# Walking the columns of every split product backwards in an attention and mixture-of-experts kernel

## The chip, the cores and the metric

The kernel runs on one core of a Trainium2 chip. The metric is the device time of one execution in microseconds (us); the median of several executions counts.

## The reference

Three stages follow each other in float32: a block-causal attention (4 batches, 8 heads, 576 positions, head size 64), a gated product chain, and a layer with eight experts of which each token uses its best two.

```python
scores = scale * np.matmul(q, k.transpose(0, 1, 3, 2))      # scale = 1/8
scores = np.where(block_i >= block_j, scores, -1e9)         # blocks of 64 positions
attn = softmax(scores);  x = np.matmul(attn, v)             # -> x: 2304 tokens x 512
h = ((x @ w1) * (x @ w2)) @ w3                              # 512 -> 1024 -> 1024
y = h @ w_out                                               # 1024 -> 512
noisy = y @ w_gate + log1p(exp(y @ w_noise)) * noise        # 8 experts, top 2 per token
out[token] += weight * (relu(y @ w1[e]) @ w2[e])            # 512 -> 1024 -> 512, per expert
```

## The kernel before

Float32 accuracy comes from splitting. `split` writes a number as a high part (rounded by ScalarE into a tile of type float32r) and a low part (what is left, by VectorE or GpSimd). `mm3` then multiplies two split operands with three matmuls that add into one accumulator tile: high by high, high by low, low by high. In every `nc.tensor.matmul(out, a, c)` the second argument is the stationary operand, 128 columns that are loaded into TensorE ahead of time (PEld in the profile), and the third is the moving operand, whose columns stream past it; each moving column makes one output column in PSUM. In `mm3` the moving operand is `c` or `d` and the output is `out`, all three with columns that lie next to each other in memory.

All calls of `mm3`, by tile name in the profile:

- `w_unit`: the product of w3 and w_out, made once, tile `m` from `pc` and `pc`, 512 columns;
- `ab`: x by w1 and by w2, tile `m` from `xh` and `pc`, 256 columns, each of the two halves of one PSUM tile in turn;
- `yout`: the gated product by the combined matrix, tile `m` from `pc` and `gt`, 512 columns;
- `ffn1`: the first layer of an expert, tile `ph` from `xt` and `pc`, 384 columns for the first three slots of 128 tokens of an expert and 256 for the other two;
- `ffn2` and `last`: the second layer, tile `ph` from `pc` and `ht`, 512 columns, and 256 in the last call.

Matmuls that don't go through `mm3` are the attention's scores (`sb`), its transposes (`tp`), its products with v (`av`), the transposes of tokens (`m` from `ident`) and the router's small products.

The work of attention, of the product chain and of the experts is interleaved by hand-written strings of steps (`FIRST`, `LATER`) and by a scheduler that orders each engine's instructions when the program is built. PSUM accumulators come from pools of two to four buffers; ScalarE and VectorE read a finished accumulator and free it. In the last 420 us or so only the experts are left: `ffn1`, `ffn2`, transposes of gathered tokens, and scattered additions to the output by GpSimd's DMA queue.

Of the kernel before, what the change touches and what calls it, by code (L numbers as in the profile page):

```python
# [464 lines left out]
class Kernel:  # L465
# [17 lines left out]
    def mm3(self, out, lh, rh, first, last):  # L483
        nc = self.nc
        (a, b), (c, d) = lh, rh
        nc.tensor.matmul(out, a, c, start=first, stop=False)  # L486
        nc.tensor.matmul(out, a, d, start=False, stop=False)  # L487
        nc.tensor.matmul(out, b, c, start=False, stop=last)  # L488
# [661 lines left out]
```

## Time and profile before

| what | value |
|---|---|
| median of 3 runs | 1082.81 us (1082.0 to 1083.41) |
| profiled execution, its own time | 1085.02 us |
| its span, first to last instruction | 1083.2 us |
| granted TensorE clock, mean | 0.986 of full speed |
| PE busy (matmuls) | 1041.1 us, 96% of the span |
| PEld busy (loads of stationary operands) | 941.3 us, 87% |
| DVE, ACT, POOL busy | 555.8, 495.6, 299.7 us |

PE is TensorE, DVE is VectorE, ACT is ScalarE and POOL is GpSimd. A matmul's duration in the trace runs from its start to the modelled end of its last column, and matmuls overlap, so that the time between the starts of two neighbours is what a matmul costs the engine; that is read from the timeline.

### The profile page before, as it was taken

The numbers are of one execution on the slowest core, as the hardware profiler recorded it, in microseconds if no ns is written. First come the engines' busy times: TensorE is split into PE (matmuls) and PEld (weight loads), VectorE is DVE, ScalarE is ACT, GpSimd is POOL, SyncE is SP. The second block draws the span as 40 slices with busy tenths as digits, with TensorE's granted clock in tenths as the row PEclk, the third lists the DMA queues.
The fourth block names the chain that finished last, engine by engine and source line by source line (L and its number), as shares of the span: only waits on it lengthen the run. The fifth ranks groups of instructions, "written<-read, shape, count | busy, mean of one in ns | idle before, by whom it ended". The sixth has DMA issues, their size and how long they took to land.

```text
span 1083.2 us, 17428 instructions
## 1 busy us (share of the span) xinstructions
PE 1041.1 (96%) x6612; PEld 941.3 (87%) x6612; DVE 555.8 (51%) x1211; ACT 495.6 (46%) x1163; POOL 299.7 (28%) x307
## 2 busy tenths in 40 slices
PE   6999898999999999999999999999999999999994
PEld 4687687898899989899999889989898989898984
DVE  7898899585755656443345443533333433334110
ACT  5775566675666656522223433543333333333110
POOL 2000123135352426231444224330404131221111
PEclk9999998999999999999999999999999999999998
DMA  8664888237542563222323455663636354442221
GB/s 278 219 209 173 232 229 156 86 112 150 169 119 72 155 178 97 77 82 59 79 51 106 101 117 168 189 187 74 157 97 157 98 147 108 118 107 36 34 30 23
DMA packets 79250, 136.34 MB, mean 126 GB/s; under 512 B 21197, under 2 KB 46773, under 8 KB 78005
## 3 DMA queue, kind: packets, MB, share of 16 engines
q1 hardware_dynamic: 68901, 113.98, 36.6%
q0 software_dynamic: 10256, 21.16, 10.9%
q8 instruction: 54, 0.88, 0.3%
q14 instruction: 39, 0.32, 0.1%
HBM read 103.92 MB, written 31.19 MB: 125 GB/s over the span
## 4 chain that ended last, share of the span: by engine, by line
PE 86%; DMA 6%; DVE 3%; ACT 1%; issue 1%; POOL 1%; SPq 0%; POOLq 0%; ACTq 0%; DVEq 0%
PE ph L486 13%; PE ph L488 13%; PE ph L487 13%; PE m L486 10%; PE m L487 10%; PE m L488 10%; PE av L702 4%; PE tp L677 4%; PE sb L647 2%; PE sb L644 2%; DMA v<-in_v_dram 2%; PE m L959 2%; DMA stg<-in_w_dram 1%; DMA qk<-in_qk_dram 1%; PE m L244 1%
## 5 line engine op out<-in xcount | busy, mean ns | idle before, releaser
L486 PE MATMUL m<-xh,pc 128*128 128x256 f32 x576 | 165.0, 289 | 1.3 <-ACT pc L477 1.0
L487 PE MATMUL m<-xh,pc 128*128 128x256 f32 x576 | 163.0, 287 | 0.0
L488 PE MATMUL m<-xh,pc 128*128 128x256 f32 x576 | 162.0, 286 | 0.6 <-DVE nm L661 0.6
L487 PE MATMUL ph<-xt,pc 128*128 128x384 f32 (+1 forms) x512 | 157.0, 307 | 0.0
L488 PE MATMUL ph<-xt,pc 128*128 128x384 f32 (+1 forms) x512 | 157.0, 307 | 0.0
L486 PE MATMUL ph<-xt,pc 128*128 128x384 f32 (+1 forms) x512 | 156.5, 307 | 0.0
L976 DVE SCALAR_TENSOR_TENSOR ht<-ph,ht 128x384 fp32r<-128x384 f32 (+1 forms) x128 | 62.1, 490 | 154.6 <-ACT ht L975 150.5
L481 DVE TENSOR_TENSOR pc<-stf,pc 128x1024 fp32r<-128x1024 f32 (+1 forms) x75 | 88.1, 1190 | 91.3 <-ACT pc L477 85.0
L486 PE MATMUL ph<-pc,ht 128*128 128x512 f32 (+1 forms) x328 | 127.9, 390 | 0.0
L487 PE MATMUL ph<-pc,ht 128*128 128x512 f32 (+1 forms) x328 | 125.9, 384 | 0.0
L488 PE MATMUL ph<-pc,ht 128*128 128x512 f32 (+1 forms) x328 | 125.9, 385 | 0.0
L1022 POOL DMA_INDIRECT out_dram<-yo,ids x39 | 63.6, 1632 | 213.4 <-ACT yo L1018 110.0
L975 ACT ACTIVATE ht<-ph 128x384 fp32r<-128x384 f32 (+1 forms) x128 | 55.5, 438 | 133.3 <-PE ph L488 131.5
L486 PEld LDWEIGHTS m<-xh,pc 128*128 128x128 f32 x576 | 110.6, 193 | 2.8 <-ACT pc L477 1.2
L663 ACT ACTIVATE pb<-sb,nm 128x288 f32<-128x288 f32 (+3 forms) x192 | 94.1, 499 | 41.0 <-DVE nm L658 13.9
L487 PEld LDWEIGHTS m<-xh,pc 128*128 128x128 f32 x576 | 110.0, 192 | 0.6
L488 PEld LDWEIGHTS m<-xh,pc 128*128 128x128 f32 x576 | 109.4, 192 | 1.0 <-DVE pc L481 0.8
L481 POOL TENSOR_TENSOR gt<-at,gt 128x256 fp32r<-128x256 f32 x72 | 58.3, 815 | 149.6 <-ACT gt L477 149.2
L487 PEld LDWEIGHTS ph<-xt,pc 128*128 128x128 f32 x512 | 96.2, 188 | 0.5 <-DVE xt L481 0.2
L486 PEld LDWEIGHTS ph<-xt,pc 128*128 128x128 f32 x512 | 96.0, 188 | 0.5
L488 PEld LDWEIGHTS ph<-xt,pc 128*128 128x128 f32 x512 | 96.2, 188 | 0.0
L658 DVE TENSOR_REDUCE nm<-sb 128x1 f32<-128x128 f32 (+2 forms) x192 | 79.2, 439 | 28.5 <-PE sb L647 27.6
(160 smaller groups left out, 2163.5 us busy)
## 6 DMA issues: line engine op xcount, KB each, us to landing
stf<-in_m_dram SPq DMA_DIRECT2D x52, 512.0 KB
qk<-in_qk_dram SPq DMA_DIRECT2D x31, 576.0 KB
stg<-in_w_dram SPq DMA_DIRECT2D x14, 1024.0 KB
x<-ev SPq DMA_DIRECT2D x32, 288.0 KB
xab<-x SPq DMA_DIRECT2D x20, 256.0 KB
yt<-y SPq DMA_DIRECT2D x18, 260.0 KB
v<-in_v_dram SPq DMA_DIRECT2D x24, 160.0 KB
out_dram<-cst SPq DMA_DIRECT2D x3, 1280.0 KB
```

The costliest lines, as they stand in the source:

```text
L481: return d, eng.tensor_tensor(l, src, r32(h), op=OP.subtract)
L486: nc.tensor.matmul(out, a, c, start=first, stop=False)
L487: nc.tensor.matmul(out, a, d, start=False, stop=False)
L488: nc.tensor.matmul(out, b, c, start=False, stop=last)
L644: nc.tensor.matmul(o, lh, c.hi[:, 1, k0:k0 + w], start=True, stop=False)
L658: nc.vector.tensor_reduce(nm[:, n:n + 1], o[:, 0:w], axis=AX, op=OP.max, negate=True)
L663: nc.scalar.activation(pb[t][:, k0:k0 + src.free_size()], src, AF.Exp, bias=nm, scale=1.0, accum_out=sums[:, h // H, t + n, h % H:h % H + 1])
L677: nc.tensor.transpose(bank[:, n * P:(n + 1) * P], pb[t][:, kt * P:(kt + 1) * P], self.ident)
L702: nc.tensor.matmul(c.av[:, o0:o0 + w], c.vv[:, kt, :], c.pt[:, i, s0:s0 + w], start=(kt == 0 and i == 0), stop=(kt == 4 and i == m - 1))
L975: a = nc.scalar.activation(hh[:, 0, f, :], ph, AF.Relu)
L976: v = nc.vector.scalar_tensor_tensor(hh[:, 1, f, :], ph, 0.0, r32(hh[:, 0, f, :]), op0=OP.max, op1=OP.subtract)
L1022: nc.gpsimd.indirect_dma_start(out=self.a["out"], out_offset=self.idx(e, i), in_=yo, in_offset=None, compute_op=OP.add)
```

## The change

One line in `mm3` turns the views of the output and of the two moving operands round, so that each of its matmuls takes its moving columns from the last to the first and writes the output columns from the last to the first too. Column j of the moving operand still makes column j of the output. The stationary operands `a` and `b` are as before. The line sits ahead of the three matmuls, so that these are L487 to L489 in the changed kernel and L486 to L488 in the kernel before; later lines shift by one too.

```diff
     def mm3(self, out, lh, rh, first, last):
         nc = self.nc
         (a, b), (c, d) = lh, rh
+        out, c, d = out[:, ::-1], c[:, ::-1], d[:, ::-1]
         nc.tensor.matmul(out, a, c, start=first, stop=False)
         nc.tensor.matmul(out, a, d, start=False, stop=False)
         nc.tensor.matmul(out, b, c, start=False, stop=last)
```

In the built program the patterns of these matmuls begin at the last column and have a step of minus one where they had a step of one. Every engine has the same instructions in the same order as before. What differs beside the patterns is which of them wait for TensorE's own semaphore (`PE_49` in the rows). On TensorE, at the start of one chunk of `ab` (`y` holds the tokens that are transposed, `pc` the weights, `gt` the gated product), the kernel before has

```order
L487 MATMUL m<-pc_77,gt 128x512
L488 MATMUL m<-pc_77,gt 128x512
L235 MATMUL m<-ident,y 128x128 [waits Activation_49]
L235 MATMUL m<-ident,y 128x128 x3
L486 MATMUL m<-xh,pc_72 128x256
L487 MATMUL m<-xh,pc_72 128x256 [waits DVE_49]
L488 MATMUL m<-xh,pc_72 128x256
```

and the changed kernel has

```order
L488 MATMUL m<-pc_77,gt 128x512
L489 MATMUL m<-pc_77,gt 128x512
L235 MATMUL m<-ident,y 128x128 [waits Activation_49]
L235 MATMUL m<-ident,y 128x128 x3
L487 MATMUL m<-xh,pc_72 128x256 [waits PE_49]
L488 MATMUL m<-xh,pc_72 128x256 [waits DVE_49]
L489 MATMUL m<-xh,pc_72 128x256
```

The first matmul into a reused accumulator has gained a wait for an earlier matmul of TensorE itself, one that stands 19 instructions ahead of it; nothing has moved. There are 25 such added waits on TensorE, and the awaited matmul stands 6 to 75 instructions ahead of the waiting one. The other way round, 28 waits of this kind are gone, as at this place among the attention's scores, where the kernel before has

```order
L486 MATMUL m<-xh,pc_67 128x256
L487 MATMUL m<-xh,pc_67 128x256
L702 MATMUL av<-pt,vv 128x320 [waits Activation_49]
L488 MATMUL m<-xh,pc_67 128x256
L644 MATMUL sb<-hi 128x288 [waits PE_49,Activation_49]
L646 LDWEIGHTS mkl
```

and the changed kernel has

```order
L487 MATMUL m<-xh,pc_67 128x256
L488 MATMUL m<-xh,pc_67 128x256
L703 MATMUL av<-pt,vv 128x320 [waits Activation_49]
L489 MATMUL m<-xh,pc_67 128x256
L645 MATMUL sb<-hi 128x288 [waits Activation_49]
L647 LDWEIGHTS mkl
```

Here the matmul of the scores has lost its wait for TensorE and keeps the one for ScalarE.

## Rows read from the trace of the kernel before

**Rows 1.** The page: busy time by engine, and 40 slices of PE and clock.

```profile
PE 1041.1 (96%) x6612; PEld 941.3 (87%) x6612; DVE 555.8 (51%) x1211; ACT 495.6 (46%) x1163; POOL 299.7 (28%) x307
...
PE   6999898999999999999999999999999999999994
...
PEclk9999998999999999999999999999999999999998
```

**Rows 2.** The page: the chain that ended last, by engine, share of the span.

```profile
PE 86%; DMA 6%; DVE 3%; ACT 1%; issue 1%; POOL 1%; SPq 0%; POOLq 0%; ACTq 0%; DVEq 0%
```

**Rows 3.** Waits, longest in total: us, times, longest; first PE's, then ACT's.

```profile
PE tp L677 <- ACT pb L663: 6.3, 7, 1.7
PE sb L644 <- ACT hi L615: 5.5, 1, 5.5
...
ACT ht L975 <- PE ph L488: 131.5, 106, 3.8
```

**Rows 4.** PE by form, the first matmul of each triple; count, busy us, mean ns.

```profile
L486 PE MATMUL m<-xh,pc 128*128 128x256 f32 x576 | 165.0, 289 | 1.3 <-ACT pc L477 1.0 <-DVE at L212 0.2
...
L486 PE MATMUL ph<-pc,ht 128*128 128x512 f32 x312 | 123.3, 396 | 0.0
...
L486 PE MATMUL ph<-xt,pc 128*128 128x384 f32 x256 | 85.5, 337 | 0.0
...
L486 PE MATMUL ph<-xt,pc 128*128 128x256 f32 x256 | 70.9, 278 | 0.0
L486 PE MATMUL m<-pc,gt 128*128 128x512 f32 x144 | 56.4, 395 | 0.0
...
L486 PE MATMUL m<-pc,pc 128*128 128x512 f32 x64 | 25.5, 412 | 0.0
...
L486 PE MATMUL ph<-pc,ht 128*128 128x256 f32 x16 | 4.5, 283 | 0.0
```

**Rows 5.** Timeline of PE, first and last of unbroken runs: start us, modelled us, form.

```profile
576.97 0.28 PE L486 MATMUL m<-xh,pc 128*128 128x256 f32 x1
...
579.72 0.28 PE L486 MATMUL m<-xh,pc 128*128 128x256 f32 x1
...
899.92 0.34 PE L486 MATMUL ph<-xt,pc 128*128 128x384 f32 x1
...
916.39 0.34 PE L488 MATMUL ph<-xt,pc 128*128 128x384 f32 x1
...
973.61 0.28 PE L486 MATMUL ph<-xt,pc 128*128 128x256 f32 x1
...
984.38 0.28 PE L488 MATMUL ph<-xt,pc 128*128 128x256 f32 x1
...
1030.62 0.39 PE L486 MATMUL ph<-pc,ht 128*128 128x512 f32 x1
...
1046.71 0.39 PE L488 MATMUL ph<-pc,ht 128*128 128x512 f32 x1
1046.94 0.28 PE L486 MATMUL ph<-xt,pc 128*128 128x256 f32 x1
...
1058.13 0.28 PE L488 MATMUL ph<-xt,pc 128*128 128x256 f32 x1
```

**Rows 6.** Windows: stretch, length, busy us by engine, granted clock, DMA share, GB/s.

```profile
460.00:462.80 2.80, 2.80 (x15) 2.80 (x14) 0.00 (x0) 0.36 (x1) 0.00 (x0) 0.50 0.12 27
577.00:579.70 2.70, 2.70 (x25) 2.70 (x24) 0.11 (x1) 0.67 (x2) 1.60 (x2) 1.00 0.04 9
```

**Rows 7.** Timeline of PE in the first of these windows, first and last row.

```profile
460.04 0.41 PE L486 MATMUL m<-xh,pc 128*128 128x256 f32 x1
...
462.81 0.41 PE L487 MATMUL m<-xh,pc 128*128 128x256 f32 x1
```

**Rows 8.** The chain at the end of the program: start us, us, what.

```profile
1065.15 4.76 DMA out_dram<-yo,ids
...
1070.66 4.44 DMA out_dram<-ye,ids
```

## The prediction

> **What bounds the kernel now.** I read the page first. PE is busy for 96% of the span, and in the 40 slices it falls under eight tenths only in the first and the last one, while the granted clock stands near full nearly everywhere [rows 1]. The chain that ended last lies on PE for 86% of its length [rows 2]. The list of waits says the same from the other side: the longest wait of PE for anybody adds up to 6.3 us, whereas ScalarE waits 131.5 us for the matmuls of `ffn1` alone [rows 3]. So TensorE is the bound, and what a matmul costs it goes straight into the time. Only from 1065 us to the end at 1083 does the chain leave it, for two scattered additions to the output of 4.8 and 4.4 us one after the other [rows 8], which the change doesn't touch.
>
> The change alters no matmul but those of `mm3`, so I need their number and what one of them costs. The listing by form gives the first matmul of each triple [rows 4]; the other two have the same counts. With three per triple:
>
> - 256 columns, from `xh` in `ab` and the few of the last call: 3 x (576 + 16) = 1776;
> - 256 columns, from `xt`: 3 x 256 = 768;
> - 384 columns, from `xt`: 3 x 256 = 768;
> - 512 columns, in `ffn2`, `yout` and `w_unit`: 3 x (312 + 144 + 64) = 1560.
>
> That is 4872 of PE's 6612 matmuls. The mean duration in that listing is no price, because matmuls overlap. The price is the distance between starts in an unbroken run, from the timeline [rows 5]. From `xh`: 576.97 to 579.72 us holds 24 matmuls, so 2.75 us over 23 steps, 119.6 ns. 384 columns: 899.92 to 916.39, 96 matmuls, 16.47 over 95, 173.4 ns. 256 columns from `xt`: 973.61 to 984.38, 96 matmuls, 10.77 over 95, 113.4 ns. 512 columns: 1030.62 to 1046.71, 72 matmuls, 16.09 over 71, 226.6 ns. Together 1776 x 119.6 + 768 x 113.4 + 768 x 173.4 + 1560 x 226.6 ns = 212 + 87 + 133 + 354 = 786 us. Nearly three quarters of the span hang on the one property that the change touches: how fast TensorE takes and writes a run of columns.
>
> **The change part by part.** It removes no instruction and adds none, and no engine's order moves. It has two effects. First, 4872 matmuls read and write with a step of minus one. Second, a few waits differ.
>
> *The waits.* 25 matmuls now also wait for an earlier matmul of TensorE itself. What is queued behind such a matmul is all of PE's program, so a wait that holds would count in full. The awaited one stands at least 6 instructions ahead. At worst a waiting matmul would have to let its direct neighbour run out: the neighbour's modelled 0.39 us less the 0.227 us after which the next one starts anyway [rows 5], 0.16 us, which 25 times is 4 us. Since TensorE works in order and the awaited matmul lies several steps back, it has normally ended by then, so I take 0 and keep 4 us as the far end. The 28 waits that are gone were of the same already answered sort: the list of waits has none of PE for PE, and the largest entry of the matmul that loses most of them, `sb` at L644, is for ScalarE [rows 3]. They give back 0.
>
> *The walk.* No matmul of the kernel before has a step other than one in a moving operand or in an output, so the trace doesn't show the price, and I bound it.
>
> From above, by the nearest row in which a column takes longer. [...] In that stretch the same matmul from `xh` starts every 213.1 ns: 460.04 to 462.81 us, 14 matmuls, 13 steps [rows 7]. That is what 256 columns cost when each takes two ticks of the full clock. Scaled by columns it makes 319.7 ns for 384 and 426.2 ns for 512. If every backward column took two ticks, the change would add 1776 x 93.5 + 768 x 99.7 + 768 x 146.3 + 1560 x 199.6 ns = 166 + 77 + 112 + 311 = 666 us.
>
> From below: half of 213.1 is 106.6 ns, what 256 columns need at full clock and nothing more; for 384 and 512 it is 159.9 and 213.1. The prices above lie 13.0, 6.8, 13.5 and 13.5 ns over that. Were walking backwards to remove all of this, it would save 1776 x 13.0 + 768 x 6.8 + 768 x 13.5 + 1560 x 13.5 ns = 23 + 5 + 10 + 21 = 60 us. I see no reason why it should: the 13 ns are there whatever the length, so they belong to the change from one matmul to the next and not to the direction within one.
>
> Between these ends I take 0. What the rows show of a matmul's price is a number of columns at the clock plus a small constant: 384 columns cost 53 to 60 ns more than 256, and 512 cost 53 ns more than 384, against 53.3 ns for 128 columns by the half-clock row. A backward walk has the same columns, the same bytes and the same neighbours in memory: two columns that follow each other still lie next to each other, and the stream reaches each stretch of memory once. Only the order within it is turned, for reads and writes alike. [...]
>
> [...]
>
> The sum is then 0 for the walk, 0 for the added waits, 0 for the lost ones. Against the profiled execution that is 1085.0 us again; its own time lies 2.2 us over the median of the runs, 1082.8 us, so I forecast 1082.8 us.
>
> **The rivals.** *Two ticks per backward column.* [...] Then PE's share grows by 666 us, no other engine can hide any of it, since all wait for PE [rows 3], and the time is 1083 + 666 = 1749 us. It is the case that ends on the slower side, and it decides as soon as a backward column costs visibly more than a tick: each tenth of a tick more would be some 67 us. For it speaks that the operands are 4 bytes wide at a column per tick of the full clock, the heaviest stream that TensorE has in this kernel; against it, that the step changes no address but the order.
>
> *A few ns per matmul more.* The trace shows that a matmul's price isn't fixed to the ns. The same 96 matmuls of `ffn1` with 256 columns cost 113.4 ns each at 973.61 us and, with 1046.94 to 1058.13 us over 95 steps, 117.8 ns in the last expert [rows 5]. If a start at the far end of a row costs such a step of 4.4 ns, all 4872 pay 21 us, and the time is 1104 us.
>
> *A few ns less.* The same step in the other direction, where the turned order meets the loads of the stationary operand more favourably, gives 1083 - 21 = 1061 us. Against both small cases: the two blocks walk in the same direction and still differ, so that the direction is not what sets this step.
>
> That the change doesn't do what it says can be left out: the built program holds the step of minus one in all these matmuls.
>
> **How the numbers follow.** No effect: 0.60. Two ticks: 0.19. A few ns more: 0.11. A few ns less: 0.10. The predicted time is that of the first, 1082.8 us. The first, third and fourth hold 0.81 together, so the range goes from 1060 to 1106 us and leaves out the rival at 1749 us; the 4 us of waits lie within it. About 0.2% (2.2 us) is what a measurement of this kernel can tell from no change. Of the first case I give 0.02 to either side for a shift of a little over that. Faster: 0.10 + 0.02 = 0.12. Same: 0.56. Slower: 0.19 + 0.11 + 0.02 = 0.32.
>
> **What would show it.** In the changed kernel the steps between starts should again be 119 to 120, 173.4, 113 to 118 and 227 ns in unbroken runs of 256 (`xh`), 384, 256 (`xt`) and 512 columns, with PE's busy time near 1041 us and no PE wait above 7 us. Steps of about 213, 320 and 426 ns at full granted clock would prove the first rival, and then PE near 100% busy. Steps that all moved by the same few ns would prove one of the small ones, and a list with PE waiting at the first matmul of an accumulator would mean the waits weren't free. The prediction is wrong if columns written or read backwards are slower at all.

## The result, and the profile after

The changed kernel takes 1094.11 us (median of 4 runs, 1093.92 to 1096.24), the kernel before beside it 1082.4 us (1081.76 to 1083.41): a ratio of 1.0105 with a 95% interval from 1.0089 to 1.0121. It is 1% slower, and the forecast of no change was wrong, though the time lies within the range. Its profiled execution has a span of 1094.4 us, 11.2 us over that of before, at a mean granted clock of 0.984 against 0.986.

The page of the changed kernel shows the same picture as [rows 1, 2], with more busy time on the engine that bounds it:

```profile
PE 1053.9 (96%) x6612; PEld 947.1 (87%) x6612; DVE 556.4 (51%) x1211; ACT 494.8 (45%) x1163; POOL 301.3 (28%) x307
...
PEclk9999898999999999999999999999999999999998
...
PE 87%; DMA 4%; DVE 3%; issue 2%; ACT 2%; SPq 1%; POOL 1%; POOLq 0%; ACTq 0%; DVEq 0%
```

PE is busy for 12.8 us more, with the same 6612 matmuls, at a clock that fell under nine tenths of full in one slice more than before. The section on the change says that every engine has the same instructions as before; that isn't quite so. The page counts 17411 instructions where that of before counts 17428: sixteen of TensorE's semaphore instructions and one of VectorE's are gone, and all others stand in the same order. The list of PE's waits (us in total, times, longest) answers to [rows 3]:

```profile
PE sb L645 <- DVE hi L615: 7.7, 3, 5.5
PE sb L645 <- ACT pb L664: 4.6, 3, 3.3
PE tp L678 <- ACT pb L664: 4.5, 5, 1.6
```

In the same list of before, `hi` stands under two engines, ACT with 5.5 us [rows 3] and DVE with

```profile
PE sb L644 <- DVE hi L614: 2.1, 2, 1.1
```

together 7.6 us, so that the 7.7 us, which pass the prediction's mark of 7 us, are the same wait and not a new one. No wait of PE for PE is in the list, and all these are waits of the attention for its own operands, of about the size they had. So the 25 added waits don't show. The listing by form answers to [rows 4], for the first matmul of each triple:

```profile
L487 PE MATMUL m<-xh,pc 128*128 128x256 f32 x576 | 165.3, 290 | 1.1 <-ACT pc L477 1.0
...
L487 PE MATMUL ph<-pc,ht 128*128 128x512 f32 x312 | 125.6, 403 | 0.0
...
L487 PE MATMUL ph<-xt,pc 128*128 128x384 f32 x256 | 86.2, 340 | 0.0
...
L487 PE MATMUL ph<-xt,pc 128*128 128x256 f32 x256 | 72.0, 282 | 0.0
L487 PE MATMUL m<-pc,gt 128*128 128x512 f32 x144 | 57.4, 402 | 0.1
...
L487 PE MATMUL m<-pc,pc 128*128 128x512 f32 x64 | 25.8, 416 | 0.0
```

The modelled mean of 512 columns rose by 4 to 7 ns and those of 384 columns and of 256 from `xt` by 3 and 4 ns, while `xh` stands within 1 ns. The price itself is again the distance between starts. From the timeline of PE, first and last of unbroken runs (start us, modelled us, form), in answer to [rows 5]:

```profile
577.52 0.28 PE L487 MATMUL m<-xh,pc 128*128 128x256 f32 x1
...
580.24 0.28 PE L487 MATMUL m<-xh,pc 128*128 128x256 f32 x1
...
982.32 0.28 PE L487 MATMUL ph<-xt,pc 128*128 128x256 f32 x1
...
993.72 0.28 PE L489 MATMUL ph<-xt,pc 128*128 128x256 f32 x1
...
1024.04 0.34 PE L487 MATMUL ph<-xt,pc 128*128 128x384 f32 x1
...
1040.72 0.34 PE L489 MATMUL ph<-xt,pc 128*128 128x384 f32 x1
1040.89 0.40 PE L487 MATMUL ph<-pc,ht 128*128 128x512 f32 x1
...
1057.46 0.40 PE L489 MATMUL ph<-pc,ht 128*128 128x512 f32 x1
```

`xh`: 24 matmuls, 2.72 us over 23 steps, 118.3 ns. 256 from `xt`: 96 matmuls, 11.40 over 95, 120.0 ns. 384: 96 matmuls, 16.68 over 95, 175.6 ns. 512: 72 matmuls, 16.57 over 71, 233.4 ns. So the steps that stood at 113.4, 173.4 and 226.6 ns grew by 6.6, 2.2 and 6.8 ns, and the one at 119.6 ns shrank by 1.3 ns.

Over the whole trace, with the mean of all steps that no wait interrupts, and `xt0`, `ht0` for the first three slots of an expert, `xt1`, `ht1` for the other two:

| moving, stationary | matmuls | before, ns | after, ns | difference, us |
|---|---|---|---|---|
| 256 `xh`, `pc` | 1728 | 119.62 | 118.58 | -1.8 |
| 256 `xt1`, `pc` | 768 | 115.06 | 119.95 | +3.8 |
| 384 `xt0`, `pc` | 768 | 173.43 | 175.55 | +1.6 |
| 512 `pc`, `gt` | 432 | 228.58 | 233.56 | +2.2 |
| 512 `pc`, `ht0` | 576 | 227.86 | 233.49 | +3.2 |
| 512 `pc`, `ht1` | 360 | 226.86 | 233.36 | +2.3 |
| 512 `pc`, `pc` | 192 | 229.69 | 233.75 | +0.8 |
| 256 `pc`, `ht1` (last call) | 48 | 119.81 | 118.34 | -0.1 |

The sum is +12.0 us against 11.2 us of span; the spans of the other three executions of the changed kernel are 1092.1 to 1092.3 us, so the two agree as well as two executions do. The steps of the split products account for the whole loss.

The theory that the runs left standing, and that most of them were made to try: a step is columns at the clock plus an extra that depends on how two reads of SBUF, that of the moving operand and that of the stationary operand, lie to each other; the direction changes that. Its rivals: the backward write into PSUM costs it; or every backward read of a matmul costs a fixed few ns; or it is the place of the tiles alone, whatever the direction.

### The profile page after: what moved, and what is told of

It reads as the page before. It is cut to its first block, busy times and chain, and to the rows that moved or that the text cites. A ratio compares the mean times of both kernels' runs of the same rounds, so it can differ in the third digit from the quotient of the medians.

```text
span 1094.4 us, 17411 instructions
## 1 busy us (share of the span) xinstructions
PE 1053.9 (96%) x6612; PEld 947.1 (87%) x6612; DVE 556.4 (51%) x1211; ACT 494.8 (45%) x1163; POOL 301.3 (28%) x307
## 4 chain that ended last, share of the span: by engine, by line
PE 87%; DMA 4%; DVE 3%; issue 2%; ACT 2%; SPq 1%; POOL 1%; POOLq 0%; ACTq 0%; DVEq 0%
PE ph L487 14%; PE ph L488 14%; PE ph L489 14%; PE m L487 10%; PE m L488 10%; PE m L489 10%; PE av L703 4%; PE tp L678 4%; PE sb L648 2%; PE sb L645 2%; PE m L960 2%; DMA v<-in_v_dram 1%; PE m L244 1%; DMA qk<-in_qk_dram 1%; PE m L235 1%
## 5 line engine op out<-in xcount | busy, mean ns | idle before, releaser
L487 PE MATMUL m<-xh,pc 128*128 128x256 f32 x576 | 165.3, 290 | 1.1 <-ACT pc L477 1.0
L488 PE MATMUL m<-xh,pc 128*128 128x256 f32 x576 | 163.3, 287 | 0.0
L489 PE MATMUL m<-xh,pc 128*128 128x256 f32 x576 | 162.4, 287 | 0.6 <-DVE nm L662 0.6
L488 PE MATMUL ph<-xt,pc 128*128 128x384 f32 (+1 forms) x512 | 159.0, 311 | 0.0
L489 PE MATMUL ph<-xt,pc 128*128 128x384 f32 (+1 forms) x512 | 158.6, 310 | 0.0
L487 PE MATMUL ph<-xt,pc 128*128 128x384 f32 (+1 forms) x512 | 158.2, 311 | 0.0
L487 PE MATMUL ph<-pc,ht 128*128 128x512 f32 (+1 forms) x328 | 130.1, 397 | 0.0
L488 PE MATMUL ph<-pc,ht 128*128 128x512 f32 (+1 forms) x328 | 128.4, 392 | 0.0
L489 PE MATMUL ph<-pc,ht 128*128 128x512 f32 (+1 forms) x328 | 128.1, 392 | 0.0
L1023 POOL DMA_INDIRECT out_dram<-yo,ids x39 | 62.3, 1597 | 205.6 <-ACT yo L1019 119.8
L487 PEld LDWEIGHTS m<-xh,pc 128*128 128x128 f32 x576 | 110.2, 192 | 2.5 <-ACT pc L477 1.2
L488 PEld LDWEIGHTS m<-xh,pc 128*128 128x128 f32 x576 | 109.5, 191 | 0.6
L489 PEld LDWEIGHTS m<-xh,pc 128*128 128x128 f32 x576 | 109.0, 191 | 1.0 <-DVE pc L481 0.8
L488 PEld LDWEIGHTS ph<-xt,pc 128*128 128x128 f32 x512 | 96.2, 188 | 0.4
L487 PEld LDWEIGHTS ph<-xt,pc 128*128 128x128 f32 x512 | 96.0, 188 | 0.5
L489 PEld LDWEIGHTS ph<-xt,pc 128*128 128x128 f32 x512 | 96.2, 188 | 0.0
L477 ACT CAST pc<-stf 128x1024 fp32r<-128x1024 f32 (+1 forms) x75 | 74.8, 1016 | 42.5 <-DMA stf<-in_m_dram 27.9
```

What stands on the lines that cost most here:

```text
L477: d = nc.scalar.copy(h, src)
L1023: nc.gpsimd.indirect_dma_start(out=self.a["out"], out_offset=self.idx(e, i), in_=yo, in_offset=None, compute_op=OP.add)
```

## The experiments

Most kernels have one run with a profile, and are read by their span and steps; where an interval stands there were several timed rounds.

**The output alone, the moving operand alone.** `mm3` takes a string that says what to turn, and only the expert layers (`ph`) pass it, "o" in the first kernel, "m" in the second.

The diff shows the two switches and the first of the three calls.

```diff
+        if "o" in w:
+            out = out[:, ::-1]
+        if "m" in w:
+            c, d = c[:, ::-1], d[:, ::-1]
...
-                         (x[:, 0, d, :], x[:, 1, d, :]), d == 0, d == 3)
+                         (x[:, 0, d, :], x[:, 1, d, :]), d == 0, d == 3, "o")
```

> In the experts' products alone (ffn1, ffn2, last: tile ph) the output columns are written from the last to the first, while the moving columns are read forwards; everything else is the kernel before. Each product's columns land in reverse order, after the routing is done. Write side theory (PSUM written backwards costs the extra): steps of 233 ns for 512 columns, 120 for 256 from xt, about 176 for 384, and a time some 11 us over before, near 1093. Read side theory (the moving stream read backwards costs it): steps of 226.7, 113 to 118 and 173.4 ns as before, time within 2 us of before.

> In the experts' products alone the moving columns are read from the last to the first, while the output is written forwards; everything else is the kernel before. Each product's columns land in reverse order, after the routing. Read side theory: 233, 120 and about 176 ns for 512, 256 and 384 columns, time near 1093 us. Write side theory: 226.7, 113 to 118 and 173.4 ns, time as before. If only both together cost anything, this run and the one with the output alone are both as before.

Output alone: 1085.38 us, span 1083.6 us. Its timeline of PE, at the ends of a run of 256 and one of 512 columns:

```profile
973.17 0.28 PE L492 MATMUL ph<-xt,pc 128*128 128x256 f32 x1
...
983.94 0.28 PE L494 MATMUL ph<-xt,pc 128*128 128x256 f32 x1
...
1030.19 0.39 PE L492 MATMUL ph<-pc,ht 128*128 128x512 f32 x1
...
1046.28 0.39 PE L494 MATMUL ph<-pc,ht 128*128 128x512 f32 x1
```

10.77 us over 95 steps and 16.09 over 71, 113.4 and 226.6 ns, are the steps of [rows 5] to the last digit. Moving operand alone: 1095.76 us, span 1094.0 us, and in the same two places:

```profile
981.50 0.28 PE L492 MATMUL ph<-xt,pc 128*128 128x256 f32 x1
...
992.90 0.28 PE L494 MATMUL ph<-xt,pc 128*128 128x256 f32 x1
...
1040.07 0.40 PE L492 MATMUL ph<-pc,ht 128*128 128x512 f32 x1
...
1056.64 0.40 PE L494 MATMUL ph<-pc,ht 128*128 128x512 f32 x1
```

That is 120.0 and 233.4 ns, the steps after the change. The terms of the `ph` forms add up to +10.8 us in the table above, and this span lies 10.8 us over that of before. For the experts' products the write into PSUM falls as a cause, and the read carries all of it; `yout` and `w_unit`, with 3.0 us of the table, were not taken apart in this way. The two runs also bear on the waits and the missing semaphore instructions: the page counts 17413 instructions with the output alone turned, at the time of before, and 17428, as before, with the moving operand alone turned, at the full loss.

**`ab` alone.** Both walks are turned in `ab` only, the form whose steps shrank; all else runs forwards.

```diff
-                           (x.h[:, 0, dt, :], x.h[:, 1, dt, :]), dt == 0, dt == 3)
+                           (x.h[:, 0, dt, :], x.h[:, 1, dt, :]), dt == 0, dt == 3, "om")
```

> Both walks reversed, but in ab alone (256 columns from xh), the one form whose step fell in the changed kernel (119.6 to 118.6 ns on average over steps under 147 ns); w_unit, yout and the experts walk forwards as before. If the price belongs to the form by itself: 1728 matmuls by 1 ns less, some 2 us faster than before, 1080 to 1081 us, and 226.7, 113 to 118 and 173.4 ns for the others. If a direction only costs or gains in company of others of the same direction: no difference from before.

1081.04 us (median of 10 runs, 1079.92 to 1082.52) against 1083.41 us, ratio 0.9982 [0.9972, 0.9992]. It beats the kernel before by about 2 us, a little less than the 0.2% that I called readable but with an interval clear of 1. Timeline of PE in it:

```profile
573.64 0.28 PE L492 MATMUL m<-xh,pc 128*128 128x256 f32 x1
...
576.37 0.28 PE L492 MATMUL m<-xh,pc 128*128 128x256 f32 x1
...
1025.98 0.39 PE L492 MATMUL ph<-pc,ht 128*128 128x512 f32 x1
...
1042.08 0.39 PE L494 MATMUL ph<-pc,ht 128*128 128x512 f32 x1
```

`xh` takes 2.73 us over 23 steps, 118.7 ns here and 118.57 over the whole trace, and 512 columns keep 226.8 ns. A fixed toll on every backward read falls too, since this one is cheaper.

**Another place for some tiles, forwards.** 64 unused bytes behind `ident` move `pc`, `xh`, `gt`, `xt1` and `ht1`, but not `xt0` and `ht0`.

```diff
-        self.ident = cp.tile([P, P], F32, name="ident")
+        self.ident = cp.tile([P, P + 16], F32, name="ident")[:, 0:P]
```

> The kernel before, walking forwards, with 64 unused bytes per partition after the identity matrix, so that all tiles allocated behind it (pc, xh, gt, xt1, ht1) lie 64 bytes further on, while xt0 and ht0, allocated from the other end, stay. Theory A, the price depends on the distance in SBUF between the moving tile and the stationary tile that is being loaded: only the pairs with changed distance move, ffn1 from xt0 (384 columns, 173.4 ns) and ffn2 with ht0 (512 columns of slots 0 to 2, 226.7 ns), by a multiple of some 6.7 ns; xh (119.6), xt1 (113 to 118) and ffn2 with ht1 stay. Theory B, the price depends on the absolute place of a tile: xt1, xh and ht1 steps change too. Theory C, direction alone sets it: nothing changes, within 1 ns, time within 2 us of before.

1084.95 us, span 1083.2 us. With `ht0`, which now lies otherwise to `pc`, the step went from 227.86 to 229.37 ns, with `xt0` from 173.43 to 173.68. Both are far less than the 6.7 ns that the expectation had. Where both tiles moved together it stayed: `ht1` 227.0, `gt` 228.9, `xh` 119.5 ns. For `ht1` of expert 5, first and last of 48 matmuls:

```profile
945.37 0.39 PE L492 MATMUL ph<-pc,ht 128*128 128x512 f32 x1
...
956.04 0.39 PE L494 MATMUL ph<-pc,ht 128*128 128x512 f32 x1
```

That is 10.67 us over 47 steps, 227.0 ns. One form doesn't fit: `xt1` moved together with `pc` and went from 115.06 to 117.77 ns. So the run leans to the distance between the two tiles and doesn't settle it.

**A ladder of places, forwards and backwards.** `xt1`, a moving operand, and `ht1`, a stationary one, begin k float32 later inside their buffers, with another k for each expert. The kernels are the same but for the direction of the `ph` products.

```diff
+        k = (0, 0, 1, 4, 8, 16, 64, 0)[e] * s
-        x = self.xt[e, s] = x[:, 0:8 * n * P].rearrange("p (m d c) -> p m d c", m=2, d=4)
+        x = self.xt[e, s] = x[:, k:k + 8 * n * P].rearrange("p (m d c) -> p m d c", m=2, d=4)
...
+            t = (self.pa if s == 0 else self.pb).tile([P, 16 * n + 128 * s], F32R, name=f"ht{s}")
+            self.ht[e, s] = t[:, k:k + 16 * n].rearrange("p (m f c) -> p m f c", m=2, f=8)
```

> All walks forward as before; in slots 3 and 4 of each expert the moving tile xt1 begins k float32 later in its own buffer, and the stationary tile ht1 likewise, with k = 0, 0, 1, 4, 8, 16, 64, 0 for experts 0 to 7 (no other tile moves between experts). Theory A, the moving stream meets the load of the next stationary tile in SBUF, so the distance of the two counts: both the ffn1 steps (256 columns, moving xt1) and the ffn2 steps (512 columns, stationary ht1) change with k, by multiples of some 6.7 ns. Theory B, only where the moving stream begins within a line of memory counts: ffn1 changes for k = 1, 4, 8 and not for 16 and 64 (64 and 256 bytes); ffn2 stays at 226.7 for all k, since its moving tile is not shifted. Theory C, direction alone: 113.4 to 118 ns and 226.7 ns for every k.

> The same ladder of k with the experts' products (ph) walked backwards in both operands. Theory A: the 120 ns of 256 columns and the 233.3 ns of 512 change with k, in both ladders. Theory B: 120 ns for k = 0, 16, 64 and another step for k = 1, 4, 8, while 512 columns stay at 233.3 for every k. Theory C: 120 and 233.3 ns for every k.

A third kernel, forwards, has k of 20, 2, 12, 24, 32, 40, 48 and 0 for `ht1`, 0, 0, 2, 12, 24, 32, 48 and 0 for `xt1`, and shifts `xh` by chunk in the same way.

> All walks forward. Three ladders of k float32 by which a tile begins later in its buffer: stationary ht1 with k = 20, 2, 12, 24, 32, 40, 48, 0 for experts 0 to 7; moving xt1 with 0, 0, 2, 12, 24, 32, 48, 0; moving xh with 24, 28, 1, 4, 8, 16, 32, 20, 0 for chunks 0 to 8. Theory A (the distance between moving stream and the load of the next stationary tile sets the price): 512 columns with ht1 show 226.7 at some k and 232 to 233 at others, as at 0, 4, 64 against 1, 8, 16 before, and k that differ by 64 agree; xh at k = 16, which then lies to pc as xt1 does (320 bytes past a multiple of 512), falls from 119.6 to 113 to 118, and chunks with k between scatter from 113 to 120. Theory B (place of the moving tile alone): 512 columns stay at 226.7 for every k of ht1, xh follows its own k only in multiples of 64 bytes. If a k of ht1 gives 220 or less for 512 columns, before was not at its best distance.

They took 1084.7 us forwards and 1091.46 backwards (before beside them: 1083.4), and 1086.9 for the third (before: 1085.25). Steps in ns, by k:

| k | 512 with `ht1`, forwards | backwards | 256 with `xt1`, forwards | backwards |
|---|---|---|---|---|
| 0 | 226.7 | 233.3 | 113.5 and 117.8 | 119.9 |
| 1 | 232.4 | 233.3 | 117.8 | 120.0 |
| 2 | 230.7 | | 121.0 | |
| 4 | 226.7 | 233.3 | 119.9 | 117.8 |
| 8 | 233.2 | 233.3 | 119.95 | 117.8 |
| 12 | 233.2 | | 113.9 | |
| 16 | 233.3 | 233.3 | 118.6 | 119.9 |
| 20 | 231.9 | | | |
| 24 | 234.2 | | 118.7 | |
| 32 | 232.4 | | 117.8 | |
| 40 | 233.3 | | | |
| 48 | 228.9 | | 119.8 | |
| 64 | 226.7 | 233.3 | 113.4 | 120.0 |

The timeline of PE of the first ladder kernel, forwards, 48 matmuls with `ht1` at k = 4 and then 48 at k = 16:

```profile
829.47 0.39 PE L492 MATMUL ph<-pc,ht 128*128 128x512 f32 x1
...
840.12 0.39 PE L494 MATMUL ph<-pc,ht 128*128 128x512 f32 x1
...
944.96 0.40 PE L492 MATMUL ph<-pc,ht 128*128 128x512 f32 x1
...
955.93 0.39 PE L494 MATMUL ph<-pc,ht 128*128 128x512 f32 x1
```

10.65 us over 47 steps, 226.6 ns, became 10.97 us, 233.4 ns, with nothing turned. In the ladder kernel that walks backwards, at the same two places:

```profile
832.01 0.40 PE L492 MATMUL ph<-pc,ht 128*128 128x512 f32 x1
...
842.98 0.40 PE L494 MATMUL ph<-pc,ht 128*128 128x512 f32 x1
...
948.95 0.40 PE L492 MATMUL ph<-pc,ht 128*128 128x512 f32 x1
...
959.91 0.40 PE L494 MATMUL ph<-pc,ht 128*128 128x512 f32 x1
```

Both take 10.96 to 10.97 us, 233.3 ns. So forwards the place of one operand moves the price of 512 columns between 226.7 and 234.2 ns, with values between, and not in multiples of 6.7 ns as the expectation had it; backwards 512 columns pay 233.3 ns at every place tried. In the `ffn2` products only the stationary tile `ht1` was moved, and the moving operand `pc` stayed. Moved by the same 64 bytes (k = 16) together with `pc`, in the kernel before this one, `ht1` kept 227.0 ns. So for 512 columns it isn't the place of the one or the other, but how the two lie to each other. A line of memory, of which one of the theories speaks, no run shows: with `pc` where it was, 512 columns pay 226.7 ns at k = 4 and 233.3 at k = 16. k = 0, 4 and 64 agree. The two table columns for `xt1` are weaker evidence: at k = 0, one and the same place, it has two prices (the last section comes back to that). None of the twelve other places beats the one that the kernel before has.

For `xh`, in the third kernel, the means of the chunks lay between 117.2 (k = 28) and 122.2 ns (k = 1), with 119.5 at k = 0 and 117.9 at k = 16, where the expectation had 113 to 118. Its larger buffer also moved `gt` by 128 bytes, and the steps with `gt` went from 228.6 to 232.4 ns, by no more than a change of place; 128 bytes are k = 32, where `ht1` has 232.4 ns too.

**384 columns backwards at other places.** As the ladder, for `xt0` with k of 0, 0, 1, 4, 8, 16, 24 and 32, the `ph` products backwards. Its buffer is 128 bytes larger and begins 128 bytes lower, so that k = 32 is the place of the changed kernel.

```diff
+        k = (0, 0, 1, 4, 8, 16, 24, 32)[e] * (1 - s)
```

> The experts' products walked backwards; moving tile xt0 (384 columns), which begins 32 bytes past a multiple of 64, starts k = 0, 0, 1, 4, 8, 16, 24, 32 float32 later for experts 0 to 7 (its buffer is 128 bytes larger). Theory A': backwards both reads of SBUF run the same way, so a distance no longer decides and the steps of 512 columns were flat; then 384 columns stay within 2 ns of 175.6 for every k. Theory B (place of the stream's first column within 64 bytes): k = 8 and 24, which begin on a multiple of 64, give 180 ns and the others less.

1096.88 us. By expert the steps are 176.7, 176.7, 177.8, 176.7, 178.3, 175.6, 176.0 and 175.5 ns: they move a little with the place and stay over the 173.4 ns of before. The 180 ns that the expectation had at k = 8 and 24 isn't there; that way of working out the price from the place falls. The other theory's 2 ns around 175.6 don't hold either, at k = 1 and 8: backwards the place still moves 384 columns by up to 2.8 ns, and at the place of the changed kernel the step is that of the changed kernel.

**Forwards at a bad place; backwards at another place.** The first kernel walks forwards and has `ht0` and `ht1` 16 float32 later for all experts. The second is the changed kernel with 32 unused bytes behind `ident`.

```diff
+            k = ((16, 16, 16, 16, 16, 16, 16, 16), (16, 16, 16, 16, 16, 16, 16, 16))[s][e]
+            t = (self.pa if s == 0 else self.pb).tile([P, 16 * n + (128 if s else 32)], F32R, name=f"ht{s}")
+            self.ht[e, s] = t[:, k:k + 16 * n].rearrange("p (m f c) -> p m f c", m=2, f=8)
```

```diff
-        self.ident = cp.tile([P, P], F32, name="ident")
+        self.ident = cp.tile([P, P + 8], F32, name="ident")[:, 0:P]
```

> All walks forward; the stationary tiles ht0 and ht1 of ffn2 begin 16 float32 (64 bytes) later in their buffers for every expert, the place at which the ladder gave 233.3 ns for ht1 (ht0's buffer grows by 128 bytes, which also moves xt0). Theory A (distance of the moving stream and the stationary load): the 936 matmuls of ffn2 with 512 columns go from 226.7 to 233 ns, some 6 us, 1088 to 1089 us, a ratio near 1.0055, without any backward walk. Theory C (direction alone): no difference from before.

> The changed kernel (all split products backward) with 32 unused bytes after the identity matrix, so that pc, xh, gt, xt1 and ht1 lie 32 bytes further on and their backward streams begin 28 instead of 60 bytes into a stretch of 64. Theory B' (backward, the first column's place within 64 bytes costs the extra): 512 columns fall from 233.3 towards 226.7 and xt1 from 120 towards 113 to 118. Theory A' (backward, both reads run the same way and the price is 233.3 at any place): 512 columns stay at 233.3 ns for ht1, gt and pc, and the time at 1094 to 1096 us.

The forward kernel takes 1092.35 us (median of 4, 1090.34 to 1093.51) against 1083.98, ratio 1.0074 [1.0049, 1.0100]. Its timeline of PE with `ht1`:

```profile
951.26 0.39 PE L492 MATMUL ph<-pc,ht 128*128 128x512 f32 x1
...
962.23 0.40 PE L494 MATMUL ph<-pc,ht 128*128 128x512 f32 x1
```

10.97 us over 47 steps, 233.4 ns. With `ht0` it is 229.4 ns: its enlarged buffer begins 128 bytes lower, so that the tile ends 64 bytes lower against `pc`, the distance that it had with the 64 bytes behind `ident`, and there too it was 229.4. With `xt0`, which that buffer moved too, it is 176.7, with `xt1` 117.8. Times their counts that makes 2.3 + 0.9 + 2.5 + 2.1 = 7.8 us against 8.0 us of span. A kernel without a single backward column loses some 70% of what the change loses. It is 3 to 4 us more than expected, and not all of it is the place's doing: `ht0` gave 1.5 ns a step and not 6.6, `xt0` wasn't in the sum of the expectation, and the 2.1 us of `xt1` came although neither `xt1` nor `pc` moved. The places that were changed account for 5.7 of the 7.8 us.

The backward one takes 1098.58 us, in one execution, 2.6 us over the far end of what was expected, which the steps of the split products don't explain; its 512 columns take 233.3 to 233.6 ns everywhere, 256 with `xt1` 119.9, 384 with `xt0` 176.0, `xh` 118.7 ns. `ht0` and `xt0` lie 32 bytes otherwise to `pc` here and pay what they paid (`xt0` 176.0 for 175.6 ns; in the ladder for 384 columns, with the same 32 bytes at k = 24, it was 176.0 too). So it isn't where the first column of a backward walk lies. Place alone, whatever the direction, has fallen with the change itself, where all tiles lie as before: the direction sets the price of a backward walk at 512 columns, and the place hardly.

## Why the prediction was wrong

*TensorE is the bound and the price of a matmul goes straight into the time:* right. Steps times counts give +12.0 us, and the span grew by 11.2.

*The waits:* right at 0. No wait of PE for PE shows, and turning the moving operand alone already gives the whole loss of the experts' products. That the change "removes no instruction" was wrong by the 17 semaphore instructions, which cost or gave nothing that shows.

*The walk:* this is the step that failed. I took 0 "between these ends", because a price was "a number of columns at the clock plus a small constant" that belonged "to the change from one matmul to the next and not to the direction within one". The constant isn't one. The prediction's own list already had it at 13.0, 6.8, 13.5 and 13.5 ns, and yet went on from "the 13 ns are there whatever the length". Over the columns at full clock (106.6, 159.9 and 213.1 ns, my estimate from half of the 213.1 ns that 256 columns take at granted clock 0.50 [rows 6, 7]) before paid 6.8, 13.5 and 13.5 ns at its good places and 13.0 with `xh`; after it is 13.3, 15.7, 20.2 and 12. For 512 columns the place of one tile moves it from 13.5 to 20.2 ns, and so does the direction of the moving operand's read. The rows of before had the hint: `xt1` at 113.4 and at 117.8 ns. I used them against the small cases, as proof that the direction doesn't set the step. They showed only that it isn't alone in setting it.

*The rivals.* "Two ticks per backward column" would have given 213, 320 and 426 ns; it falls, since no run shows a backward column at two ticks: the dearest mean steps of backward forms are 120.0 ns for 256 columns, 178.3 for 384 and 233.8 for 512. "A few ns per matmul more", at 1104 us by its price of 4.4 ns for all 4872, comes nearest, but its own sign, steps that all move by the same few ns, isn't there. Measured, the change is -1.5 to +6.5 ns by form and 2.5 ns on average; the 1728 matmuls of `xh` gained. Its price came from two blocks that walk the same way and read `xt1` from the same place, so from neither of the causes found here. That it put 1094 us inside the range is luck.

*The same bytes in another order.* I took 0 for reads and writes alike, since a backward walk has the same columns, the same bytes and the same neighbours. For the write that held in the experts' products: with a backward output 512 columns take 226.6 ns as before, and a step of minus one in PSUM costs nothing there. For the read by the moving operand it didn't: the steps of 512 columns in the experts' products grew by 5.6 to 6.5 ns.

What is shown: in the experts' products the loss lies in the read of the moving operand (a span of 1094.0 us with it turned, 1083.6 with the output turned); forwards the price of 512 columns depends on how the moving and the stationary tile lie to each other (226.7 to 234.2 ns); backwards 512 columns pay the dearer price wherever they were put (233.3 to 233.8 ns). What is only argued: that the two reads hinder each other inside SBUF, and that a forward walk can be at a place where they don't while a backward one can't. Why a backward read is dearer stays open: no run turns the stationary operand's read, or shows in which direction it goes.

## What to carry to other kernels

When TensorE is the bound and its matmuls follow each other without a gap, the step between starts is worth reading per form and per tile: 3% of it (226.7 against 233.3 ns) can hang on where two tiles lie. Tiles that lie 64 to 128 bytes elsewhere went with 0.7% more time here, about three quarters of it in the steps of these tiles, with no work added. A constant read from one layout isn't a constant until another layout has shown it too. Turn a walk round, or shift a tile, for one form at a time and keep what its own step says: `ab` alone gained 2 us where all together lost 11.

## What was not expected of the hardware

At granted clock 1.00 a step costs more than the estimate for its columns, by an amount that changes with layout and direction: for 512 columns mostly 226.7 or 233.3 ns, 13.6 and 20.2 ns over the estimated 213.1, with means between (228.9 to 232.4 ns) at some places; for 256 between 113.4 and 122.2 ns, 6.8 to 15.6 over 106.6. At granted clock 0.50 next to no extra is left, by an estimate from [rows 5]: 512 columns cost 53.2 ns more than 384, which makes 53.2 ns for 128 columns at full clock and 212.8 ns for 256 at half of it, and the row has 213.1 ns [rows 7].

Moving only the stationary operand by 64 bytes changes the step of 512 columns by 6.6 ns, from 226.7 to 233.3; moved together with the moving operand it changes nothing (227.0). So the price of a matmul depends here on the place of the one tile against the other. That the two reads get into each other's way somewhere would fit; no run shows that they do, or where.

And a price can differ at one and the same place: in expert 0 `xt1` took 117.8 ns a step in the kernel before and 113.5 ns with only the output turned, from the same addresses. It happens within one execution too. `piece` gives experts 1, 4 and 7 the same weight tiles, and `xt1` lies at one address for all experts, yet in the kernel before experts 1 and 4 show

```profile
688.06 0.28 PE L486 MATMUL ph<-xt,pc 128*128 128x256 f32 x1
...
699.25 0.28 PE L488 MATMUL ph<-xt,pc 128*128 128x256 f32 x1
...
859.53 0.28 PE L486 MATMUL ph<-xt,pc 128*128 128x256 f32 x1
...
870.30 0.28 PE L488 MATMUL ph<-xt,pc 128*128 128x256 f32 x1
```

11.19 and 10.77 us over 95 steps, 117.8 and 113.4 ns, and expert 7 is back at 117.8 [rows 5]. What ran just before differs: experts 1 and 7 follow directly on `ffn2`, at 117.8, and experts 2 to 6 directly on the products of 384 columns, at 113.4; in the two forward kernels where `xt0` or `pc` had moved, and with them the place of those 384 columns against `pc`, all eight take 117.8, and `xt1` didn't move against `pc` in either. So a run may keep a price that its start gave it. That would explain the one form that didn't fit above, and it is a guess that no run was made to test.
